# Reciprocals of the norm taken at application, and the last chunk of x loaded early, in a two-layer attention and feed-forward kernel

## The chip, the cores and the metric

One core of one Trainium2 chip. The metric is the device time of one execution in microseconds (us). Executions of one kernel agree within 0.3%, and the granted TensorE clock rounds to 1.00 in all runs whose clock is on record (nine of them are listed at 0.999; the last experiment comes to them), so all runs compared here are of one state. The kernel was well tuned before: the question is about 0.1% of its time, which makes it a good exercise in finding the one place where a tuned kernel still waits.

## The reference, cut to what matters

```python
x = A_x                                                    # 2048 tokens, 1024 wide, bf16
x = x + _A_ref(_layernorm(x), A_wqkv, A_wo)    # dilated local attention, 32 heads, 8 keys each
x = x + _B_ref(_layernorm(x), B_w1, B_w3, B_w2)            # gated feed-forward, 3584 wide
x = x + _A_ref(_layernorm(x), A_wqkv, A_wo)    # the same two once more, the same weights
x = x + _B_ref(_layernorm(x), B_w1, B_w3, B_w2)

def _layernorm(x, axis=-1, eps=1e-5):
    m = jnp.mean(x, axis=axis, keepdims=True)
    v = jnp.var(x, axis=axis, keepdims=True)
    return (x - m) / jnp.sqrt(v + eps)
```

## The kernel before

The tokens are cut into 4 chunks of 512, each into two halves (r = 0, 1) of two 128-token tiles. TensorE (PE) does the projections q, k, v of chunk 0, 1, 2, 3 in turn, then the output projection and the feed-forward. The attention itself, with its 8 keys per query, is elementwise work on VectorE (DVE): a long chain for each half chunk, whose result `oT` PE then needs as weights of the output projection (`po`).

While the program is built, a small plan is kept: `now` holds estimated clocks of PE, DVE and ScalarE (ACT), and `x_at` the estimated arrival of each chunk of x. Norm and attention steps are put into DVE's fixed instruction order where the plan says that DVE has time, and output-projection tiles into PE's where the plan says that `oT` is ready. In the traces each engine keeps to its list: PE, DVE and ACT of `load_only` (below) ran in the same order as in the kernel before, although DVE's waits differ by up to 8.9 us.

```python
now = dict(pe=23.6, dve=15.0, act=24.5, table=None)
x_at = [12.5, 21.0, 24.0, 36.0]            # the plan's arrival of x, per chunk

def background(until):                     # fill DVE's order up to time `until`: norms first
    while True:
        for queue in (norms, attention):
            s = head(queue)
            if s is not None and max(now["dve"], s[1]) + s[0] <= until:
                take(queue)
                break
        else:
            return

def norm_stats(key, c, r):
    # ... buffers cut
    def aggregate(i):
        nc.vector.bn_aggr(mv[:, i, :], st[:, i, :, :])
        if i == 1:
            nc.scalar.activation(sd[:], mv[:, :, 1], ACTF.Sqrt, bias=epst[:])
            at["sd"] = act(0.3, now["dve"] + 0.1, "sqrt")
    for i in range(2):
        for hh in range(2):
            yield 0.61, x_at[c], lambda: stats(i, hh)
        yield 0.12, 0.0, lambda: aggregate(i)
    yield 0.10, at["sd"], lambda: nc.vector.reciprocal(rstd[:], sd[:])
    moments[key, r] = mv, rstd

def norm_apply(key, c, r):                 # (x - mean) * rstd, then a DMA transpose to xnT
    # ... cut
        nc.vector.tensor_scalar(xn[:], x_sb[:, c * TPC + j, :], mv[:, i, 0:1], rstd[:, i:i + 1],
                                op0=ALU.subtract, op1=ALU.mult)
        nc.sync.dma_start_transpose(out=xnT[:, :, j * P:(j + 1) * P], in_=xn[:])

# loads at the start, all issued by SyncE (SP), in this order (cut):
#   x of chunk 0 between q's weights; k's weights; x(1); x(2)
# later, in the k projection of chunk 0:
then = (lambda: (load_weight(), load_weight()), None, lambda: load_x(3))   # v's weights ... x(3)

def between(hold, must=False):             # called after every two projection groups
    flush()
    while o_queue and (must or oT_at.get((o_queue[0][0], o_queue[0][1] // 2), 1e9) + 0.3 <= now["pe"]):
        o_tile()                           # 16 matmuls po, oT as weights
        if not must:
            break
    # ... cut
```

"x(3)" below is the load of chunk 3 of x, "the plan" is the bookkeeping above, and a "group" is the 8 matmuls that fill one PSUM bank.

Of the kernel before, what the change touches and what calls it, by code (L numbers as in the profile page):

```python
# [7 lines left out]
FP32 = mybir.dt.float32  # L8
# [7 lines left out]
def kernel(  # L16
# [13 lines left out]
    nc = tc.nc  # L30
    cfg = dict(cfg or {})
    P = 128
# [6 lines left out]
    NCH = S // CH  # L39
    TPC = CH // P  # L40
# [42 lines left out]
    now = dict(pe=23.6, dve=15.0, act=24.5, table=None)  # L83
    units = [(l, c) for l in range(2) for c in range(NCH)]
    norms, attention = [], []
    x_at = [12.5, 21.0, 24.0, 36.0]
    xnT_at, norm_left, qkv_at, oT_at, o_todo = {}, {}, {}, {}, {}

    def pe(n, ready=0.0):
# [7 lines left out]
    def act(cost, ready=0.0, table=None):  # L97
        t = max(now["act"], ready)
        if table is not None and table != now["table"]:
            now["table"] = table  # L100
            t += TABLE
        now["act"] = t + cost
        return now["act"] + 0.1
# [76 lines left out]
    def norm_stats(key, c, r):  # L180

        st = small.tile([P, 2, 2, 6], FP32, name="st")
        mv = small.tile([P, 2, 2], FP32, name="mv", bufs=4)
        sd = small.tile([P, 2], FP32, name="sd")
        rstd = small.tile([P, 2], FP32, name="rstd", bufs=4)
        at = {}

        def stats(i, hh):
            nc.vector.bn_stats(st[:, i, hh, :], x_sb[:, c * TPC + 2 * r + i, hh * 512:(hh + 1) * 512])  # L189

        def aggregate(i):
            nc.vector.bn_aggr(mv[:, i, :], st[:, i, :, :])
            if i == 1:
                nc.scalar.activation(sd[:], mv[:, :, 1], ACTF.Sqrt, bias=epst[:])
                at["sd"] = act(0.3, now["dve"] + 0.1, "sqrt")

        for i in range(2):
            for hh in range(2):
                yield 0.61, x_at[c], lambda: stats(i, hh)
            yield 0.12, 0.0, lambda: aggregate(i)  # L200
        yield 0.10, at["sd"], lambda: nc.vector.reciprocal(rstd[:], sd[:])
        moments[key, r] = mv, rstd

    def norm_apply(key, c, r):

        if key not in xnTs:
            xnTs[key] = xtp.tile([P, KT, CH], BF16, name="xnT")
        xnT = xnTs[key]
        mv, rstd = moments[key, r]

        def apply(i):
            j = 2 * r + i
            xn = xnp.tile([P, D], BF16, name="xn")
            nc.vector.tensor_scalar(xn[:], x_sb[:, c * TPC + j, :], mv[:, i, 0:1], rstd[:, i:i + 1],  # L214
                                    op0=ALU.subtract, op1=ALU.mult)
            with hp():
                nc.sync.dma_start_transpose(out=xnT[:, :, j * P:(j + 1) * P], in_=xn[:])
            xnT_at[key] = now["dve"] + DMA
            norm_left[key] = norm_left.get(key, TPC) - 1

        for i in range(2):
            yield 0.47, 0.0, lambda: apply(i)

    moments = {}

    def queue_norm(key, c, r, parts=(norm_stats, norm_apply)):
        for part in parts:
            norms.append([part(key, c, r), None])

    def first_q(ws, loads):  # L230

# [17 lines left out]
        load_tile(3, 0, D, nc.sync)  # L249
        load_weight()  # L250
        load_weight()
        load_x(1)
        load_x(2)
        preload = small.tile([P, 1], FP32, name="preload", bufs=1)
        nc.scalar.activation(preload[:], epst[:], ACTF.Sqrt)

# [283 lines left out]
    def o_tile():  # L540

        l, n = o_queue.pop(0)
        h, j = n // 2, n % 2
        force(attention, lambda: (l, h) in oT_at)
        oT = oTs[l, h]
        for hh in range(2):
            ps = bank("po")
            for t in range(KT):
                nc.tensor.matmul(ps[:], lhsT=oT[:, t, j * P:(j + 1) * P], rhs=wo[:, t, hh * 512:(hh + 1) * 512],  # L549
                                 start=(t == 0), stop=(t == KT - 1))  # L550
            r = pe(KT, oT_at[l, h] + 0.2)
            xs = x_sb[:, n, hh * 512:(hh + 1) * 512]
            background(r)
            nc.vector.tensor_tensor(xs, xs, ps[:], op=ALU.add)  # L554
            dve(0.64, r)
        o_todo[l, h] -= 1
        if j == 1:
            norm_queue.append((("B", l, n // TPC), n // TPC, h % R))

    def between(hold, must=False):  # L560

# [45 lines left out]
    def b_stage(u, hold):  # L607

        l, c = units[u]
        last = l == 1  # L610
        ready = ready_norm(("B", l, c))
        xnT = xnTs[("B", l, c)]
        for (f0, f1) in fsplits:
            lastsplit = (f1 == fsplits[-1][1])
            for g0 in range(f0, f1, FG):
                gn = min(FG, f1 - g0)
                w1t, w3t = weight("w1"), weight("w3")
                for fi in range(gn):
                    f = g0 + fi
                    slack = 1.0 if f < f1 - 2 else -0.5  # L620
                    if f < f1 - 1:
                        between(hold)
                    else:
                        flush()
                    if f == 8 and 1 <= u and u + 3 < len(units):
                        lq, cq = units[u + 3]
                        for r in range(R):
                            queue_norm(("Q", lq, cq), cq, r)
                    pg = bank("pg")
                    for kk in range(KT):  # L630
                        nc.tensor.matmul(pg[:], lhsT=w1t[:, kk, fi * P:(fi + 1) * P], rhs=xnT[:, kk, :],  # L631
                                         start=(kk == 0), stop=(kk == KT - 1))
                    r = pe(KT, ready)
                    sg = sgp.tile([P, CH], BF16, name="sg")
                    nc.scalar.activation(sg[:], pg[:], ACTF.Silu)  # L635
                    ts = act(0.6, r, "silu")
                    pu = bank("pu")
                    for kk in range(KT):
                        nc.tensor.matmul(pu[:], lhsT=w3t[:, kk, fi * P:(fi + 1) * P], rhs=xnT[:, kk, :],  # L639
                                         start=(kk == 0), stop=(kk == KT - 1))  # L640
                    r = max(pe(KT), ts)
                    background(r + slack)
                    nc.vector.tensor_tensor(hT[:, f - f0, :], sg[:], pu[:], op=ALU.mult)  # L643
                    th = dve(0.64, r)
                release(2)
            for hh in range(2):
                w2ts = [weight("w2") for g0 in range(f0, f1, 8)]
                for j in range(TPC):
                    n = c * TPC + j
                    final = u == len(units) - 1 and lastsplit and hh == 1 and j == TPC - 1  # L650
                    step = 256 if final else 512
                    for q0 in range(0, 512, step):
                        acc = psum.tile([P, step], FP32, name="acc", tag="mm")
                        for f in range(f0, f1):
                            nc.tensor.matmul(acc[:], lhsT=hT[:, f - f0, j * P:(j + 1) * P],  # L655
                                             rhs=w2ts[(f - f0) // 8][:, (f - f0) % 8, q0:q0 + step],
                                             start=(f == f0), stop=(f == f1 - 1))
                        if q0 == 0:
                            pe(f1 - f0 - 1)
                            r = pe(1, th)  # L660
                            background(r + 1.0)
                            dve(0.64, r)
                        o0 = hh * 512 + q0
                        xs = x_sb[:, n, o0:o0 + step]
                        nc.vector.tensor_tensor(xs, xs, acc[:], op=ALU.add)  # L665
                        if last and lastsplit:
                            nc.sync.dma_start(xout[:, n, o0:o0 + step], xs)
                    if j == TPC - 1:
                        release(2)
                    between(hold and not lastsplit, lastsplit and hh == 0 and j == 1 and not hold)  # L670
# [10 lines left out]

    first_q(w_tiles[0:2], load_wq)
    xnT_at["Q", 0, 0], norm_left["Q", 0, 0] = now["pe"], 0
    queue_norm(("Q", 0, 1), 1, 0)
    queue_norm(("Q", 0, 1), 1, 1)
    for c in (2, 3):
        for r in range(R):
            queue_norm(("Q", 0, c), c, r, (norm_stats,))
    for c in range(NCH):
        for which in range(3):  # L690
            if c == NCH - 1 and which == 0:
# [4 lines left out]
            if c == 0 and which == 0:  # L696
                continue
            if c == 0 and which == 1:
                then = (lambda: (load_weight(), load_weight()), None, lambda: load_x(3))
            if c == 2 and which == 0:  # L700
                then = (None, None, lambda: nc.sync.dma_start(wo[:], wo_v))
            if c == 2 and which == 1:
# [2 lines left out]
            if c == NCH - 1:  # L705
                release(2)
            if which == 0 and 1 <= c < NCH - 1:
                for r in range(R):
                    queue_norm(("Q", 0, c + 1), c + 1, r, (norm_apply,))
    used[0] = 6  # L710
    for u, (l, c) in enumerate(units):
        if u + 1 < len(units):
# [41 lines left out]
```

## Time and profile before

| | before |
|---|---|
| time, median of the first 3 runs | 1619.39 us (1618.79 to 1619.96) |
| profiled span | 1616.9 us |
| PE busy | 1610.4 us, 100% |
| DVE busy | 1166.3 us, 72% |
| granted clock | 1.00 |

First the part of the page that follows the chain that ended last back from the end, as shares by engine and by line:

```profile
PE 91%; DVE 7%; DMA 1%; SPq 0%; issue 0%; ACT 0%; ACTq 0%; DVEq 0%
PE acc L655 24%; PE pu L639 24%; PE pg L631 24%; PE ps L588 12%; PE po L549 6%; DVE pr L421 1%; DVE tm L481 1%; DVE tm L355 1%; DVE pr L355 1%; PE pq L287 1%; DMA wqkv<-in_A_wqkv_dram 1%; DVE st L189 1%; DMA x_sb<-in_A_x_dram 0%; DVE At L465 0%; DVE L L445 0%; DVE xn L214 0%
```

PE bounds the kernel, but 7% of the chain is DVE: somewhere PE waited, and the chain left PE there and went back along DVE's attention (`pr`, `tm`). "PE busy 100%" would hide this. The Trainium skill warns of it: "Perfetto Trace Analysis", Identifying the Most-Contended Engine, says that matmul busy share is no measure of the distance to the roofline, because matmuls are pipelined. This trace agrees that the share misleads. The page's reason is that such matmuls look smaller in the trace; here each looks longer than its turn: a 128x512 matmul is listed at 379 ns, while the next one starts after 216 ns (215.8 on average from the first gate matmul to the end), so a gap of up to 163 ns leaves no mark in the busy time. I therefore read the distances between matmul starts in the trace. After the first k projection at 23.59 us all are 215 to 226 ns, nearly all 215 or 216 (a few half-wide matmuls at the very end follow each other faster), but two: 1422 ns at 162.81 us and 661 ns at 164.23 us. What they exceed 216 ns by, 1206 + 445 = 1651 ns, is all that PE loses between 23.59 us and its last matmul.

The view of busy time per stretch finds the same place (stretch, its length, then busy us and instruction count of PE, weight loads, DVE, ACT, POOL; clock; DMA share; GB/s):

```profile
140.00:160.00 20.00, 20.00 (x94) 12.38 (x93) 19.83 (x37) 5.78 (x10) 0.00 (x0) 1.00 0.25 81
160.00:180.00 20.00, 18.69 (x86) 10.64 (x85) 19.46 (x36) 3.83 (x8) 0.00 (x0) 1.00 0.73 209
```

The timeline of the kernel before at that place (start us, duration, engine, line, operation, output<-input; in brackets the idle time before and what ended it):

```profile
161.73 1.46 PE L549 MATMUL po<-wo,oT 128*128 128x512 bf16 x6
...
163.89 0.28 DVE L357 TENSOR_TENSOR oT<-tm 128x256 bf16<-128x256 bf16 x1
...
164.23 0.39 PE L549 MATMUL po<-wo,oT 128*128 128x512 bf16 x1 [1.04 <-DVE oT L357]
164.54 0.29 DVE L357 TENSOR_TENSOR oT<-tm 128x256 bf16<-128x256 bf16 x1
...
164.89 0.39 PE L549 MATMUL po<-wo,oT 128*128 128x512 bf16 x1 [0.27 <-DVE oT L357]
```

PE begins the third output tile at 161.73 us, has six of the eight slices of `oT` of the second attention half, and waits for the last two, which DVE writes at 163.89 and 164.54 us. Why is DVE late? Further back in the same view, where attention starts:

```profile
41.05 0.47 SPq L674 DMA_DIRECT2D x_sb<-in_A_x_dram  x1
...
47.75 1.28 DVE L189 BATCH_NORM_STATS2 st<-x_sb 128x6 f32<-128x512 bf16 x2 [8.88 <-DMA x_sb<-in_A_x_dram]
...
54.58 1.20 DVE L421 TENSOR_TENSOR pr<-qT,kT 128x2048 bf16<-128x2048 bf16 x1
```

x(3) is issued at 41.05 us, DVE stands idle for 8.88 us until it lands, takes chunk 3's statistics, and only then starts attention, at 54.58 us. From there to 164.8 us it is busy almost without a break.

### The profile page before, as it was taken

How to read it: one execution, taken by the hardware profiler on the slowest of the kernel's cores; microseconds unless marked ns; L12 is line 12 of the kernel's file. 1: busy time of each engine (PE TensorE's matmuls, PEld its weight loads, DVE VectorE, ACT ScalarE, POOL GpSimd, SP SyncE). 2: the span in 40 equal slices, each digit the busy share in tenths (PEclk: the TensorE clock that was granted, in tenths of full speed). 3: DMA queues.
4: the chain of work that ended last, by engine and by line, in shares of the span. 5: the costliest groups of instructions: out<-in, count | busy, mean ns of one | idle time of the engine just before them, and what ended most of it. 6: DMA issues, size and time to landing. Idle time of an engine off the chain costs nothing.

```text
span 1616.9 us, 19388 instructions
## 1 busy us (share of the span) xinstructions
PE 1610.4 (100%) x7672; PEld 805.8 (50%) x7672; DVE 1166.3 (72%) x1964; ACT 353.2 (22%) x549; POOL 1.9 (0%) x12
## 2 busy tenths in 40 slices
PE   9999999999999999999999999999999999999999
PEld 7666544444445544455444554445544444444444
DVE  5799998989899898988898549983599832222212
ACT  4333311212112230222302123021230212011110
POOL 0000000000000000000000000000000000000000
PEclk9999999999999999999999999999999999999999
DMA  9565865466538664567563776638675265436440
GB/s 303 145 187 166 254 188 163 134 189 195 170 105 235 222 200 126 170 209 235 145 211 122 211 241 165 191 102 257 212 222 158 91 196 169 143 107 218 156 130 27
DMA packets 336396, 285.84 MB, mean 177 GB/s; under 512 B 69680, under 2 KB 318896, under 8 KB 336176
## 3 DMA queue, kind: packets, MB, share of 16 engines
q1 hardware_dynamic: 336160, 284.46, 58.0%
q8 instruction: 60, 0.98, 0.3%
q14 instruction: 32, 0.26, 0.1%
q10 hardware_dynamic: 144, 0.13, 0.0%
HBM read 239.47 MB, written 29.36 MB: 166 GB/s over the span
## 4 chain that ended last, share of the span: by engine, by line
PE 91%; DVE 7%; DMA 1%; SPq 0%; issue 0%; ACT 0%; ACTq 0%; DVEq 0%
PE acc L655 24%; PE pu L639 24%; PE pg L631 24%; PE ps L588 12%; PE po L549 6%; DVE pr L421 1%; DVE tm L481 1%; DVE tm L355 1%; DVE pr L355 1%; PE pq L287 1%; DMA wqkv<-in_A_wqkv_dram 1%; DVE st L189 1%; DMA x_sb<-in_A_x_dram 0%; DVE At L465 0%; DVE L L445 0%; DVE xn L214 0%
## 5 line engine op out<-in xcount | busy, mean ns | idle before, releaser
L639 PE MATMUL pu<-xnT,w3t 128*128 128x512 bf16 x1792 | 423.3, 379 | 0.0
L631 PE MATMUL pg<-xnT,w1t 128*128 128x512 bf16 x1792 | 423.3, 379 | 0.0
L655 PE MATMUL acc<-w2t,hT 128*128 128x512 bf16 (+1 forms) x1804 | 389.7, 378 | 0.0
L588 PE MATMUL ps<-xnT,wqkv 128*128 128x512 bf16 x1472 | 319.2, 379 | 0.0
L635 ACT ACTIVATE sg<-pg 128x512 bf16<-128x512 f32 x224 | 133.9, 598 | 805.7 <-PE pg L631 802.6
L643 DVE TENSOR_TENSOR hT<-sg,pu 128x512 bf16<-128x512 bf16 x224 | 152.5, 681 | 193.4 <-PE pu L639 186.2
L655 PEld LDWEIGHTS <-hT 128*128 128x128 bf16 x1804 | 176.5, 98 | 210.5
L631 PEld LDWEIGHTS <-w1t 128*128 128x128 bf16 x1792 | 175.3, 98 | 211.4 <-issue 0.2
L639 PEld LDWEIGHTS <-w3t 128*128 128x128 bf16 x1792 | 175.3, 98 | 211.5
L588 PEld LDWEIGHTS <-wqkv 128*128 128x128 bf16 x1472 | 211.1, 143 | 106.7
L421 DVE TENSOR_TENSOR pr<-qT,kT 128x2048 bf16<-128x2048 bf16 x128 | 155.8, 1217 | 81.8 <-DMA kT<-qkv_d 81.8
L665 DVE TENSOR_TENSOR x_sb<-x_sb,acc 128x512 bf16<-128x512 bf16 x129 | 87.4, 677 | 105.5 <-PE acc L655 105.5
L481 DVE TENSOR_TENSOR tm<-At,vT 128x2048 bf16<-128x2048 bf16 x128 | 155.8, 1217 | 0.2
L592 ACT CAST sgt<-ps 128x512 bf16<-128x512 f32 x184 | 104.7, 589 | 219.2 <-PE ps L588 180.4
L355 DVE TENSOR_TENSOR tm<-tm 128x1024 bf16<-128x1024 bf16 (+1 forms) x256 | 137.4, 551 | 0.5
L355 DVE TENSOR_TENSOR pr<-pr 128x1024 bf16<-128x1024 bf16 (+1 forms) x256 | 136.9, 551 | 0.5
L549 PE MATMUL po<-wo,oT 128*128 128x512 bf16 x512 | 116.1, 379 | 1.3 <-DVE oT L357 1.3
L189 DVE BATCH_NORM_STATS2 st<-x_sb 128x6 f32<-128x512 bf16 x120 | 75.8, 671 | 15.5 <-DMA x_sb<-in_A_x_dram 15.5
L549 PEld LDWEIGHTS <-oT 128*128 128x128 bf16 x512 | 50.0, 98 | 61.8 <-DVE oT L357 2.1
L554 DVE TENSOR_TENSOR x_sb<-x_sb,po 128x512 bf16<-128x512 bf16 x64 | 43.3, 684 | 25.9 <-PE po L549 25.8
L635 ACT ACT_TABLE_LOAD x31 | 39.8, 1283 | 48.7 <-PE pg L631 48.5
L465 DVE STREAM_TRANSPOSE At<-AeT 128x2048 bf16<-128x2048 bf16 x16 | 36.9, 2305 | 0.1
(83 smaller groups left out, 402.9 us busy)
## 6 DMA issues: line engine op xcount, KB each, us to landing
w1t<-in_B_w_dram SPq DMA_DIRECT2D x56, 1024.0 KB, 5.5
w3t<-in_B_w_dram SPq DMA_DIRECT2D x56, 1024.0 KB, 8.0
w2t<-in_B_w_dram SPq DMA_DIRECT2D x48, 1024.0 KB, 5.7
wqkv<-in_A_wqkv_dram SPq DMA_DIRECT2D x28, 1024.0 KB, 6.8
qkv_d<-sgt SPq DMA_DIRECT2D x92, 256.0 KB, 3.6
qT<-qkv_d SPq DMA_DIRECT2D x16, 512.0 KB, 8.7
w2t<-in_B_w_dram SPq DMA_DIRECT2D x16, 512.0 KB, 5.2
kT<-qkv_d SPq DMA_DIRECT2D x14, 544.0 KB, 9.4
```

Source lines behind the costliest of these rows:

```text
L189: nc.vector.bn_stats(st[:, i, hh, :], x_sb[:, c * TPC + 2 * r + i, hh * 512:(hh + 1) * 512])
L355: nc.vector.tensor_tensor(b[:, 0:m, :], b[:, 0:m, :], b[:, m:2 * m, :], op=ALU.add)
L421: V.tensor_tensor(pr[:], qT[:], kT[:, :, k0:k0 + TCH], op=ALU.mult)
L481: V.tensor_tensor(tm[:], At[:], win, op=ALU.mult)
L549: nc.tensor.matmul(ps[:], lhsT=oT[:, t, j * P:(j + 1) * P], rhs=wo[:, t, hh * 512:(hh + 1) * 512], start=(t == 0), stop=(t == KT - 1))
L588: nc.tensor.matmul(ps[:], lhsT=ws[kk // KH][:, kk % KH, t::KT], rhs=xnT[:, kk, :], start=(kk == 0), stop=(kk == KT - 1))
L592: nc.scalar.copy(sgt[:, t - t0, :], ps[:])
L631: nc.tensor.matmul(pg[:], lhsT=w1t[:, kk, fi * P:(fi + 1) * P], rhs=xnT[:, kk, :], start=(kk == 0), stop=(kk == KT - 1))
L635: nc.scalar.activation(sg[:], pg[:], ACTF.Silu)
L639: nc.tensor.matmul(pu[:], lhsT=w3t[:, kk, fi * P:(fi + 1) * P], rhs=xnT[:, kk, :], start=(kk == 0), stop=(kk == KT - 1))
L643: nc.vector.tensor_tensor(hT[:, f - f0, :], sg[:], pu[:], op=ALU.mult)
L655: nc.tensor.matmul(acc[:], lhsT=hT[:, f - f0, j * P:(j + 1) * P], rhs=w2ts[(f - f0) // 8][:, (f - f0) % 8, q0:q0 + step], start=(f == f0), ...
```

## The change

Its intent: x of all chunks loads right behind k's weights, so that x(3) is there when DVE comes to it; and the reciprocal of the standard deviation, which waits for ScalarE's square root, is taken only when the norm is applied, after the statistics of both halves, so that DVE need not wait for the square root in between. The plan's arrival times follow.

```diff
-    x_at = [12.5, 21.0, 24.0, 36.0]
+    x_at = [12.5, 21.5, 25.0, 28.5]
@@ norm_stats
             if i == 1:
                 nc.scalar.activation(sd[:], mv[:, :, 1], ACTF.Sqrt, bias=epst[:])
-                at["sd"] = act(0.3, now["dve"] + 0.1, "sqrt")
+                moments[key, r] = mv, sd, act(0.3, now["dve"] + 0.1, "sqrt")
...
-        yield 0.10, at["sd"], lambda: nc.vector.reciprocal(rstd[:], sd[:])
-        moments[key, r] = mv, rstd
@@ norm_apply
-        mv, rstd = moments[key, r]
+        mv, sd, ready = moments[key, r]
+        rstd = small.tile([P, 2], FP32, name="rstd")
...
+        yield 0.10, ready, lambda: nc.vector.reciprocal(rstd[:], sd[:])
         for i in range(2):
             yield 0.47, 0.0, lambda: apply(i)
@@ queue_norm: all halves' statistics, then all halves' applications
-    def queue_norm(key, c, r, parts=(norm_stats, norm_apply)):
+    def queue_norm(key, c, rs, parts=(norm_stats, norm_apply)):
         for part in parts:
-            norms.append([part(key, c, r), None])
+            for r in rs:
+                norms.append([part(key, c, r), None])
@@ first_q
-        load_x(1)
-        load_x(2)
+        for c in range(1, NCH):
+            load_x(c)
@@ the k projection of chunk 0
-                then = (lambda: (load_weight(), load_weight()), None, lambda: load_x(3))
+                then = (lambda: (load_weight(), load_weight()),)
... (callers of queue_norm, cut)
```

More of the change, by code (lines that the diff above doesn't have):

```diff
@@ L183, in norm_stats @@
         mv = small.tile([P, 2, 2], FP32, name="mv", bufs=4)
-        sd = small.tile([P, 2], FP32, name="sd")
-        rstd = small.tile([P, 2], FP32, name="rstd", bufs=4)
-        at = {}
+        sd = small.tile([P, 2], FP32, name="sd", bufs=4)
         def stats(i, hh):
@@ L557, in o_tile @@
         if j == 1:
-            norm_queue.append((("B", l, n // TPC), n // TPC, h % R))
+            norm_queue.append((("B", l, n // TPC), n // TPC, (h % R,)))
     def between(hold, must=False):
@@ L626, in b_stage @@
                         lq, cq = units[u + 3]
-                        for r in range(R):
-                            queue_norm(("Q", lq, cq), cq, r)
+                        queue_norm(("Q", lq, cq), cq, range(R))
                     pg = bank("pg")
@@ L683 @@
     xnT_at["Q", 0, 0], norm_left["Q", 0, 0] = now["pe"], 0
-    queue_norm(("Q", 0, 1), 1, 0)
-    queue_norm(("Q", 0, 1), 1, 1)
+    queue_norm(("Q", 0, 1), 1, range(R))
     for c in (2, 3):
-        for r in range(R):
-            queue_norm(("Q", 0, c), c, r, (norm_stats,))
+        queue_norm(("Q", 0, c), c, range(R), (norm_stats,))
     for c in range(NCH):
@@ L707 @@
             if which == 0 and 1 <= c < NCH - 1:
-                for r in range(R):
-                    queue_norm(("Q", 0, c + 1), c + 1, r, (norm_apply,))
+                queue_norm(("Q", 0, c + 1), c + 1, range(R), (norm_apply,))
     used[0] = 6
```

## The prediction

> What bounds the kernel now. TensorE, almost alone. In 20-us windows PE is busy 20.00 of 20 us in all but three, and the granted clock is 1.00. "Busy" flatters pipelined matmuls (the Trainium skill, "Perfetto Trace Analysis", Identifying the Most-Contended Engine), so I read start distances: after the start phase a 128x512 matmul follows another every 216 ns, though each is listed at 379 ns. Between 23.6 us (first k projection) and 191.0 us (first gate matmul) stand 768 such matmuls: 165.8 us of work in 167.4 us, so 1.6 us of stall. The timeline puts it in one place: PE po at 162.8 and 164.2 us, released by DVE oT (the list of waits: 1.3 us in two pieces; window 160-180 is busy 18.69). From 191 us to the last matmul at 1613.7 us no start distance exceeds 240 ns. The loads that PE waits for before 23.6 us stay where they are. So about 1.65 us (0.1%) can be won.
>
> Why oT is late. The first two attention halves are a DVE chain that starts at 54.6 us. DVE idled before it: 8.9 us until x of chunk 3, issued at 41.05 and landed at 47.7 us (timeline), and some 4 us in small waits, mostly of the reciprocal for ScalarE's square root (over the whole run 5.8 us in 11 waits). From 60 to 180 us DVE is about 97% busy.
>
> What the change does.
> - x of chunk 3 is issued at about 11 us, not 41. DMA moved 380-400 GB/s until 22 us, then was nearly idle for 1.5 us; 1 MB costs about 2.7 us of queue: x(3) lands by 25-28 us, and the 8.9 us idle goes.
> - Reciprocals (158 ns each, 30 in both kernels) move behind both halves' statistics: some 3 us of early waits go.
> - The instruction order shows the schedule following: attention begins right after the last statistics; two residual adds and one half's norm of the feed-forward (5.3 us of DVE) fall behind the second half's oT. The second pair of output-projection tiles moves ahead by 48 projection matmuls (10.4 us), to about 151.4 us.
> - Chunk 1's DMA transposes now stand four in a row behind v's weights, delaying the load of qT.
>
> Estimate: DVE statistics end near 40.5 us; qT lands at 43-46 us, so attention starts 9-11 us earlier. Second-half oT ends at 164.8 - 5.3 + 0.6 - (9 to 11) = 149-151 us. PE needs it by 152.9 us: the stall goes, with a margin of only 2-4 us. v's weights, needed at 37.4 us, were there by about 36; no transpose runs ahead of them now, so no new stall.
>
> Predicted: 1617.8 us, range 1617.0 to 1619.6 (8 in 10). Chances: faster by over 2% 0.002, within 2% 0.994, slower by over 2% 0.004.
>
> Right if: one matmul chain at 216 ns from 23.6 us to the end, no PE wait for oT; first gate matmul at 189.4 us, not 191.0; attention's first product near 44 us; DVE's wait for x after 40 us gone; DVE busy time (1166 us) and matmul count (7672) unchanged.
>
> Wrong if: qT's load is held up behind the transposes past 48 us, so that the output tiles, moved 10 us forward, still wait for oT (time unchanged); x(3) delays chunk 1's x or k's weights (due at 23.6 us); v's weights land after 37.4 us; a new stall appears later, where all output tiles moved two gate groups forward.

## The result, and the profile after

| | before | after |
|---|---|---|
| time, median of 6 runs | 1619.33 us (1618.79 to 1620.9) | 1617.24 us (1616.94 to 1617.71) |
| ratio | | 0.9986 (95%: 0.9973 to 0.9999) |
| profiled span | 1616.9 us | 1615.4 us |
| PE lost between first k projection and last matmul | 1.65 us | 0 |
| first k projection starts | 23.59 us | 23.74 us |
| attention starts on DVE | 54.58 us | 46.04 us |

A ratio here is the mean time of one kernel's fast runs over that of the other's of the same rounds, so it is not quite the ratio of the medians quoted. The change makes the kernel 0.14% faster.

One trap has to be cleared first. The trace of after holds 7525 matmul records where before has 7672, and from the 300th on every 49th start distance in it is 431 or 432 ns (the first 442): twice 216. The weight loads are all there (7672). So every 50th matmul record is missing, and no matmul took longer. It shows in PE's busy column, 19.89 where 20.00 stood before, in both stretches alike:

```profile
140.00:160.00 20.00, 19.89 (x93) 11.25 (x93) 19.86 (x38) 4.88 (x8) 0.00 (x0) 1.00 0.18 58
160.00:180.00 20.00, 19.89 (x92) 12.91 (x93) 19.53 (x37) 5.84 (x11) 0.00 (x0) 1.00 0.88 222
```

Apart from that beat no start distance after 23.74 us is over 216 ns. The share of DVE in the chain has fallen from 7% to 3%, and cut to the first 200 us the chain holds no DVE work at all any more:

```profile
PE 94%; DVE 3%; DMA 1%; issue 1%; SPq 0%; ACT 0%; DVEq 0%
PE acc L653 24%; PE pu L637 23%; PE pg L629 22%; PE ps L587 19%; PE po L548 6%; PE pq L286 1%; DMA kT<-qkv_d 1%; DMA wqkv<-in_A_wqkv_dram 1%; DVE pr L420 1%; DVE pr L354 0%; DVE hT L641 0%; DVE x_sb L553 0%; DVE st L187 0%; DVE tm L354 0%; DVE tm L480 0%
```

(Most of what is left of DVE there lies between 950 and 1006 us. The start distances show no wait of PE in that stretch, so this part of the chain is not a cost: a chain followed back by semaphores can leave the engine that bounds at a place where it was not waiting.)

The third output tile in the timeline of after:

```profile
150.48 0.29 DVE L356 TENSOR_TENSOR oT<-tm 128x256 bf16<-128x256 bf16 x1
...
151.14 0.29 DVE L356 TENSOR_TENSOR oT<-tm 128x256 bf16<-128x256 bf16 x1
...
151.53 3.19 PE L548 MATMUL po<-wo,oT 128*128 128x512 bf16 x13
```

The tile now stands at 151.53 us, 10.2 us earlier, and no bracket follows it: the last slice of `oT` is ready at 151.43 us, and PE comes to it with its eighth matmul, at 151.53 + 7 x 0.216 = 153.04 us. The margin is 1.6 us. Where attention starts:

```profile
38.82 1.28 SPq L214 DMA_TRANSPOSE xnT<-xn  x1
39.79 0.21 DVE L190 BATCH_NORM_AGGREGATE mv<-st 128x2 f32<-128x12 f32 x1
...
40.78 0.63 SPq L386 DMA_DIRECT2D qT<-qkv_d  x1
...
46.04 1.23 DVE L420 TENSOR_TENSOR pr<-qT,kT 128x2048 bf16<-128x2048 bf16 x1 [6.04 <-DMA qT<-qkv_d]
```

The wait for x(3) is gone: DVE is done with all statistics at 40.0 us. But a new wait of 6.04 us stands in its place, for `qT`, whose load SyncE could issue only after four DMA transposes in a row, which took its queue 10.5 us (29.58 to 40.1 us). In the kernel before the four took 10.0 us in all as well, but `qT`'s load stood behind two of them there (issued at 34.25 us) and stands behind all four now (40.78 us): its place in SyncE's list is what changed. Attention starts 8.5 us earlier, where DVE's own work would have allowed some 14.

The two profiles differ by 1.50 us: 1.65 us of stall, less 0.15 us of a slower start phase. The medians differ by 2.09 us. The rest is how the runs scatter: the profiled run of before took 1618.72 us, 0.6 us under its median, that of after 1617.19 us, at its median. The last experiment comes back to this.

### The profile page after: what moved, and what is told of

It reads as the page before. It is cut to its first block, busy times and chain, and to the rows that moved or that the text cites. A ratio compares the mean times of both kernels' runs of the same rounds, so it can differ in the third digit from the quotient of the medians.

```text
span 1615.4 us, 19241 instructions
## 1 busy us (share of the span) xinstructions
PE 1601.8 (99%) x7525; PEld 805.9 (50%) x7672; DVE 1164.2 (72%) x1964; ACT 353.2 (22%) x549; POOL 1.9 (0%) x12
## 4 chain that ended last, share of the span: by engine, by line
PE 94%; DVE 3%; DMA 1%; issue 1%; SPq 0%; ACT 0%; DVEq 0%
PE acc L653 24%; PE pu L637 23%; PE pg L629 22%; PE ps L587 19%; PE po L548 6%; PE pq L286 1%; DMA kT<-qkv_d 1%; DMA wqkv<-in_A_wqkv_dram 1%; DVE pr L420 1%; DVE pr L354 0%; DVE hT L641 0%; DVE x_sb L553 0%; DVE st L187 0%; DVE tm L354 0%; DVE tm L480 0%
## 5 line engine op out<-in xcount | busy, mean ns | idle before, releaser
L442 DVE STREAM_TRANSPOSE psmT<-psm 128x2048 bf16<-128x2048 bf16 x16 | 36.9, 2307 | 0.2
```

## The experiments

Theory 1: the whole gain is the stall of PE for `oT`. `oT` was late because x(3) was late, and anything that gets `oT` to PE before PE's turn is worth 1.65 us and no more. Rival 1: the waits for ScalarE's square root, which the reciprocals' move takes away, are what counted. Rival 2: what counted is the place of the output tiles in PE's order, which the plan moved.

| kernel | median us (5 runs) | ratio to before (95%) | attention starts | PE lost after the first k projection |
|---|---|---|---|---|
| `aa_before` | 1619.27 | 1.0001 (0.9989 to 1.0014) | 54.5 | 1.64 us, for oT |
| `load_only` | 1616.91 | 0.9984 (0.9971 to 0.9996) | 45.4 | 0 |
| `norm_only` | 1625.26 | 1.0036 (1.0023 to 1.005) | 56.4 | 7.3 us: 3.4 for oT, 3.9 new |
| `load_old_plan` | 1618.7 | 0.9994 (0.9981 to 1.0006) | 47.5 | 1.7 us, for v's weights |
| `true_x3` | 1617.32 | 0.9987 (0.9973 to 1.0001) | 40.9 | 0 |
| `hold_po` | 1617.2 | 0.9987 (0.9974 to 0.9999) | 55.0 | 0 |
| `old_plan_v_early` | 1617.0 | 0.9985 (0.9973 to 0.9998) | 43.9 | 0 |
| `early_tile1` | 1616.99 | 0.9985 (0.9972 to 0.9997) | 45.5 | 0 |

The intervals are as wide as the effects, because before itself scatters; so the verdicts rest on the stalls in the traces, with the medians beside them. The last column is what the start distances exceed 216 ns by, summed. All runs were correct. First came the top four, on one chip, against 9 runs of before (median 1619.28 us).

### aa_before: the kernel before once more

No edit. Expected:

> The kernel before, unchanged, as a measure of noise: ratio 1.000, span about 1617 us, one PE stall of 1.4 to 2.3 us near 163 us, released by DVE oT. The two medians on record differ by 2.1 us while the two traces differ by 1.5 us. If the median here is again near 1619.3 and its trace shows a stall of about 2.2 us, the size of the stall varies from run to run; if the stall is again 1.65 us, the rest of the 2.1 us is elsewhere (the start phase) or noise.

Measured: 1619.27 us, the same stall (1407 and 660 ns at 162.85 and 164.26 us). The noise of a median is well under 0.5 us, and 1.64 us of stall repeats.

### load_only: only x(3) moves

```diff
 # on the kernel before
-        load_x(1)
-        load_x(2)
+        for c in range(1, NCH):
+            load_x(c)
...
-                then = (lambda: (load_weight(), load_weight()), None, lambda: load_x(3))
+                then = (lambda: (load_weight(), load_weight()),)
-    x_at = [12.5, 21.0, 24.0, 36.0]
+    x_at = [12.5, 21.5, 25.0, 28.5]
```

The new `x_at` alone was only built: it leaves the order of every engine as it is, because in the old norm code the plan's waits for the square root cover it. So this kernel differs from before in SyncE's list alone; the two traces show the same order on every other engine.

> Only x(3)'s load moves (and the plan's arrival constants, which by themselves leave the program unchanged); PE, DVE and ACT orders are those of the kernel before. Theory 1 (PE waits only for a late oT, and DVE was late because x(3) was late): DVE's 8.9 us wait goes, attention starts at about 45.7 us instead of 54.6, second-half oT ends near 156 us, PE needs it at 163 us: no stall, time -1.6 us, first gate matmul at about 189.4 us. Rival 1 (the waits for ScalarE's square root are what mattered): no change in time.

Measured: 1616.91 us, no stall. It has the whole gain of the change, with the reciprocals where they were. Its statistics still pay the square-root waits, 4.2 us in six pieces, yet attention starts at 45.44 us, 0.6 us before after's. Where attention starts:

```profile
45.35 0.17 DVE L201 RECIPROCAL rstd<-sd 128x2 f32<-128x2 f32 x1 [0.42 <-ACT sd L194]
45.44 1.20 DVE L421 TENSOR_TENSOR pr<-qT,kT 128x2048 bf16<-128x2048 bf16 x1
```

No wait for `qT` stands before the first product: here the transposes do not stand four in a row, and SyncE issues `qT` at 33.93 us. In after, what the reciprocals' move saved on DVE was lost again to SyncE's queue. Rival 1 falls.

### norm_only: only the reciprocals move

The kernel after, with the loads and `x_at` of before (the two diffs above, reversed).

> Only the reciprocals move; x(3) loads where it did. The instruction order puts the second pair of output tiles one group (16 matmuls, 3.45 us) earlier on PE than in the kernel before. Theory 1: x(3) still lands at 47 to 49 us, attention starts at 54 to 55 us, oT ends at 163.5 to 165 us, PE now needs it at about 159.7 us: stall of 4 to 5 us, so 2.2 to 3.4 us slower than before. Rival 1: 1.6 us faster.

Measured: 1625.26 us, 6 us slower than before: the direction of theory 1, but more than its 2.2 to 3.4 us. PE's waits from 20 to 170 us in the list of waits (engine, line, waited for: us in total, times, longest):

```profile
PE po L548 <- DVE oT L356: 3.1, 2, 2.8
...
PE ps L587 <- ACT sgt L591: 2.3, 2, 1.4
...
PE ps L587 <- DMA wqkv<-in_A_wqkv_dram: 1.0, 1, 1.0
```

The first line is what was expected: 3.4 us by start distances, against 4 to 5. The other two were not. v's weights came too late (1.3 us by start distances, near 38 us), and PE's projections (`ps`) twice waited for ScalarE to empty their PSUM bank into a staging tile, `sgt` (2.7 us together, near 53 and 84 us). The timeline of SyncE shows where the first comes from: in this build one transpose stands ahead of the first store `sgt` and of v's weights in SyncE's list, and with both halves' statistics first, its input comes only at 27.8 us instead of 25.5. All behind it slip: v's weights are issued at 29.86 us instead of 28.29, and x(3) at 43.23 instead of 41.05. For x(3) DVE then waits 15.66 us. The timeline of ScalarE shows where the other two come from:

```profile
53.69 0.30 ACT L192 ACTIVATE sd<-mv,epst 128x2 f32<-128x2 f32 x1 [14.80 <-DVE mv L190]
...
83.75 0.63 ACT L439 ACTIVATE E<-L 128x512 bf16<-128x512 f32 x1 [11.58 <-DVE L L438]
```

Each time ScalarE stood in its list at an instruction whose input DVE had not made yet: at the square root of chunk 3's statistics, which wait for x(3), and at the exponential of the late attention. Its copies to `sgt` stood behind (53.89 and 84.29 us), and PE went on at 54.51 and 84.91 us. So the late x(3) reaches PE by two ways here, through `oT` and through ScalarE's list. `load_old_plan`, the next run, has the same orders on PE, DVE and ScalarE with x(3) early, and both waits are gone.

### load_old_plan: both code changes, the old arrival constants

The kernel after, with `x_at = [12.5, 21.0, 24.0, 36.0]`. PE, DVE and ACT have the same orders as in `norm_only`; only x(3)'s load differs.

> The changed kernel with the old arrival constants: both code changes, and the same PE, DVE and ACT orders as norm_only; only the load of x(3) differs from norm_only. Theory 1: attention starts near 46 us, oT ends near 156.7 us, needed at 159.7 us: no stall, time as the changed kernel, 1.6 us under before and some 4 us under norm_only. If the new position of the output tiles on PE were what gained, it would be as norm_only.

Measured: 1618.7 us. Against `norm_only`, the load of x(3) alone is worth 6.6 us by the medians (5.6 by start distances, 0.5 by an earlier first k projection), and the stall for `oT` is gone (last slice at 158.37 + 0.29 us, needed at 161.4). But the time is not after's: PE lost 1.7 us near 38 us. SyncE's list in the timeline, and the wait that results:

```profile
27.62 1.34 SPq L214 DMA_TRANSPOSE xnT<-xn  x1
...
29.63 1.08 SPq L511 DMA_DIRECT2D wqkv<-in_A_wqkv_dram  x2
30.82 10.26 SPq L214 DMA_TRANSPOSE xnT<-xn  x3
...
39.84 1.52 PE L587 MATMUL ps<-xnT,wqkv 128*128 128x512 bf16 x6 [1.49 <-DMA wqkv<-in_A_wqkv_dram]
```

In after, the new constants put all four transposes behind v's weights, which are issued at 28.43 us there, and PE does not wait. So this change of `x_at`, which looks like bookkeeping, carries 1.7 us of stall in the new code, and nothing in the old (there another change of it does: `true_x3`).

### old_plan_v_early: v's weights out of the transpose's way

The second four kernels ran on one chip against 9 runs of before (median 1619.04 us).

```diff
 # on load_old_plan
-        for c in range(1, NCH):
-            load_x(c)
+        load_x(1)
+        load_weight()
+        load_weight()
+        load_x(2)
+        load_x(3)
...
-                then = (lambda: (load_weight(), load_weight()),)
+                then = ()
```

> load_old_plan with v's weights issued between x(1) and x(2), not behind the first DMA transpose. Theory 3: the 1.7 us that PE waited near 38 us in load_old_plan was for v's weights, held in the issuing queue behind a transpose whose input came later than before. It goes, nothing replaces it: 1.6 us faster than load_old_plan (1618.7), so about 1617.0. If the wait was for ScalarE or PSUM, it stays.

Measured: 1617.0 us, no stall at all, 1.7 us under `load_old_plan`. So it was v's weights. Their second half had landed 2.2 us later in `load_old_plan` than in after: it was issued 1.2 us later (30.16 against 28.94 us), behind the transpose, and took 9.7 us instead of 8.7 to land. What lengthened the flight was not tested.

### true_x3: one number of the plan, nothing loads earlier

```diff
 # on the kernel before
-    x_at = [12.5, 21.0, 24.0, 36.0]
+    x_at = [12.5, 21.0, 24.0, 47.7]
```

> The kernel before with one number of the plan changed: x(3) is said to arrive at 47.7 us (as its trace shows) instead of 36. No load moves. The built order has the same PE order for the output tiles, but DVE now starts attention after chunk 2's statistics and takes chunk 3's later. Theory 1: DVE fills the 8.9 us hole with attention from about 41 us (when qT lands); oT ends at about 157 to 160 us, PE needs it at 163: no stall, 1.6 to 2.2 us faster than before. If it is the early load as such that gains, no change.

Measured: 1617.32 us, no stall. x(3) is issued at 41.31 us, as late as ever, and the orders of PE and SyncE are those of before, but DVE's is another (and ScalarE's square roots go with it): DVE fills the hole with attention and takes chunk 3's statistics later. In the timeline:

```profile
40.87 1.23 DVE L421 TENSOR_TENSOR pr<-qT,kT 128x2048 bf16<-128x2048 bf16 x1 [1.90 <-DMA qT<-qkv_d]
41.31 0.46 SPq L674 DMA_DIRECT2D x_sb<-in_A_x_dram  x1
...
49.57 1.28 DVE L189 BATCH_NORM_STATS2 st<-x_sb 128x6 f32<-128x512 bf16 x2
```

The second half's `oT` ends at 160.01 + 0.29 us; PE comes to that tile at 161.84. The kernel before put x(3) 11.7 us too early in its own plan. Telling the plan the truth is worth as much as making the plan true.

### hold_po: the output tiles later in PE's order

```diff
 # on the kernel before
-    ... oT_at.get(..., 1e9) + 0.3 <= now["pe"]
+    ... oT_at.get(..., 1e9) + 3.3 <= now["pe"]
```

> The kernel before, with output-projection tiles placed on PE only when the plan has oT ready 3.3 us earlier (0.3 before). The second pair of tiles goes back by one group, 3.45 us. DVE is as late as before (oT ends near 164.8 us), but PE comes to it at 165.2 us. Rival 2 (the stall is a matter of where the plan puts the tiles, not of DVE's lateness): no stall, 1.6 to 2.2 us faster than before, with attention still starting at 54.6 us. If only an earlier oT helps: no change.

Measured: 1617.2 us, no stall, with DVE as late as before. The timeline at the third output tile:

```profile
165.03 0.29 DVE L357 TENSOR_TENSOR oT<-tm 128x256 bf16<-128x256 bf16 x1
...
165.41 1.89 PE L549 MATMUL po<-wo,oT 128*128 128x512 bf16 x8
```

`oT` is even 0.5 us later than in the kernel before, but the tile stands one step (16 matmuls) later on PE, which has other projections to do meanwhile. (The instructions of DVE, ScalarE and SyncE that follow the output tiles move with them; attention starts at 55.0 us, no earlier than before.) So theory 1 was too narrow: "oT is late" means late for the place that the plan gave the tile. Either side can move. Rival 2 is half right: moving the tile is enough, but not needed (`load_only` left it where it was).

### early_tile1: a try at the start phase

With the stall gone, PE's remaining waits stand before 12 us, where q's first weights land. `load_only`, with rows of tile 1's products set between tile 0's last rows (cut to its core):

```diff
-        for kk in range(KT):                     # tile 0, then tile 1 as a whole
-            ...
+        for kk in range(4):
+            row(0, accs, kk)
+        turn(1, xn)                              # transposes of tile 1
+        ...
+        for j, kk in ((0, 4), (0, 5), (1, 0), (0, 6), (1, 1), (0, 7)):
+            row(j, (accs, accs1)[j], kk)
```

> load_only, with the first q projection re-ordered: part of tile 1's products stands between tile 0's last ones, so that PE has work while q's last weights land (waits at 8.8 to 11.4 us of 0.1 to 0.8 us in the traces so far). Expected: 0.1 to 0.7 us faster than load_only (1616.9), so 1616.2 to 1616.8; no stall elsewhere; slower if the shift makes PE wait for ScalarE's copies of the transposes.

Measured: 1616.99 us against 1616.91 for `load_only`, from another chip session: no gain. Its first k projection starts at 23.55 us, between 23.43 (`load_only`) and 23.74 us (after), which run the old order. PE still waits for the fifth piece of q's weights (0.28 us at 9.89 us), where the edit has only moved tile 1's transposes ahead of it and its products behind it. The start phase varied by 0.4 us (23.43 to 23.82 us) between traces that run the same PE instructions in it, and this edit cannot be told from that.

### aa_look1, aa_look2, aa_look3: why before scatters more

Of 29 timed runs of the kernel before (6, then 9 and 5, then 9), six took 1620.85 to 1621.3 us, and the others 1618.13 to 1619.96. The 31 runs of kernels without a stall (after, `load_only`, `true_x3`, `hold_po`, `old_plan_v_early`, `early_tile1`) all lie between 1616.36 and 1617.71.

> The kernel before again, one look. So far 6 of its 29 timed runs took 1620.8 to 1621.3 us instead of 1618.1 to 1620, and none of 31 runs of the kernels without a stall for oT left 1616.4 to 1617.7 us. If a look catches such a run: theory 1 expects the stall near 163 us to be about 3.6 us instead of 1.65 (something ahead of oT came 2 us later); a rival (start phase, final store) expects the same 1.65 us stall and the 2 us elsewhere. If it catches none, this stays open.

> As the look before it: an unusual run shows whether its extra 2 us stand at the stall for oT.

> As the look before it: an unusual run shows whether its extra 2 us stand at the stall for oT.

Measured: 1618.79, 1618.87 and 1619.28 us; none of the 2 us kind. The third is of use all the same. In its timeline x(3) lands 0.5 us later than in the other traces of before:

```profile
41.19 0.46 SPq L674 DMA_DIRECT2D x_sb<-in_A_x_dram  x1
48.24 1.29 DVE L189 BATCH_NORM_STATS2 st<-x_sb 128x6 f32<-128x512 bf16 x2 [9.30 <-DMA x_sb<-in_A_x_dram]
...
55.07 1.20 DVE L421 TENSOR_TENSOR pr<-qT,kT 128x2048 bf16<-128x2048 bf16 x1
```

Attention starts 0.5 us later (55.07 against 54.58 us), the stall is 2.1 us instead of 1.65 (1896 + 659 - 2 x 216 ns), and the span is 0.56 us longer (1617.47 against 1616.91). In this trace the delay of x(3) goes through to the time nearly one to one, as PE waits for `oT`; with a margin it should not. One trace cannot show how often this happens, but it would account for scatter of half a microsecond in before, and for medians that gained more (2.1 us) than the stall of the profiled run (1.65 us).

The six runs that were 2 us longer were not caught in a trace. They may be the same thing at a larger size, since no kernel without the stall has them. But the record holds a rival: the five of them whose clock is listed have 0.999, all other listed runs of before 1.000. Rounded so, by estimate 0.999 stands for 0.8 to 2.4 us of lost clock (0.05 to 0.15% of 1619 us), enough for the 2 us. Four of the five runs of `norm_only` have 0.999 too, and no run without the stall for `oT` has. So the lower clock goes with that stall; whether it is the cause of the longer time or only its mark stays open.

## Why the prediction was right or wrong, point by point

- The size of the prize was right. 1.65 us of stall, one place, nothing else after 23.6 us: after has no stall, the first gate matmul moved from 191.02 to 189.51 us (predicted: 189.4), and 1617.24 us lies in the range of 1617.0 to 1619.6, 0.6 us under the 1617.8 named. The 0.6 us is a term that I left out: the three runs that I subtracted from had a median 0.67 us above the run that left the profile, and part of that scatter seems to come through the same stall (`aa_look3`, one trace) and to go with it.
- "Why oT is late" was right as to x(3): its load alone brings the whole gain (`load_only`). It was incomplete as to the cause. DVE's lateness cost time only because the plan had placed the output tile by a wrong arrival of x(3); correcting that number (`true_x3`) or moving the tile by one step (`hold_po`) gains the same with no load moved.
- "some 3 us of early waits go" is the step that failed in its consequence. The waits of the reciprocals did go (DVE's statistics ended at 40.0 us, predicted 40.5), but the time became a 6.04 us wait for `qT`. I had seen the four transposes in front of `qT`'s load and put its landing at 43 to 46 us; it was 46.0, at the late end. That term was mis-sized: the row of transposes held SyncE for 10.5 us. So attention started 8.5 us earlier and not the predicted 9 to 11, and the margin was 1.6 us and not 2 to 4. The reciprocals' move brought nothing to the time (after is not faster than `load_only`), and without the early load and the new constants it costs 6 us (`norm_only`).
- "no transpose runs ahead of them now, so no new stall" (v's weights) was right for after, by little: their second half landed at 37.6 us, and the matmul that needs it starts at 38.4. (In before it landed at 37.4 us, and not "by about 36".) In `load_old_plan`, with one transpose ahead, they were late by 1.7 us.
- "x(3) lands by 25-28 us" cannot be read off directly, as nobody waited for it; chunk 3's statistics began without a wait at 34.3 us. DVE busy time fell only from 1166.3 to 1164.2 us, as a change that removes no work should do. The matmul count is 7672 only by the weight loads, because the trace lost matmul records.

## What to carry to other kernels

When one engine bounds a kernel, look for the few places where it starts late, and ask of each both questions: can the input come earlier, and can the engine do something else first? Here one load, one corrected number in the build-time plan and one later slot in PE's order each removed the same stall of 1.65 us, so they cannot add up. And treat the issuing queue as an engine with an order of its own: an instruction that waits there for its input, like a transpose whose statistics were just moved back, delays every load behind it, so a gain on one engine can come back as a wait for a DMA on another.

## What the Trainium skill lacked or had wrong

- "TensorE: Matmul & The Clock Gate", Back-to-back issue gap, gives about 131 ns per matmul of N=512 as the sustained rate of a stream of weight loads and matmuls, and calls 216 ns the gap of an isolated one. In the trace of before such a stream of some 6580 pairs ran at 215.8 ns on average, nearly each at 215 or 216. The same page, in its step-by-step part on the phases of a matmul, has 216 ns for back-to-back matmuls; that is what these runs show.
- "DMA: Bandwidth & Descriptors", Issuing engines are not separate DMA queues, says that the sequencer's time to start a DMA is usually small relative to the DMA itself. Here four DMA transposes of 256 KB in a row kept SyncE's queue busy for 10.5 us (3.45, 4.23, 1.26 and 1.28 us, with their inputs ready), against a median of 4.8 us from issue to landing, and DVE waited 6 us for `qT`, whose load stood behind them. The page counts sequencer cycles of a transpose by itself (in its table on trn3 B0, beside previous generations), but nothing there tells when one holds the queue for 1.3 us and when for 4.2.
- "Perfetto Trace Analysis" does not say that matmul records can be missing at a regular beat: in the trace of after (and in those of `aa_look1` to `aa_look3`), every 50th, 147 of 7672, each showing as a start distance of 432 ns = 2 x 216. Counting the weight loads, or halving the odd distance, tells such a gap from a stall.
